# Attention and a long convolution on one core: scores in rounds of three head pairs over three double-bank buffers, and one PSUM bank for all other matrix work

## The chip, the cores and the metric

The kernel runs on one NeuronCore of a Trainium2 chip. The metric is the device time of one execution in microseconds. The kernel before took 1288.97 us (median of three runs, 1287.18 to 1289.61).

## The reference, cut to what matters

Two independent results are put side by side. The first is a state-space convolution: for each of 576 channels a kernel `K` of 2048 taps is generated from complex parameters, and the input `u` is convolved with it by a Fourier transform of double length. The second is attention with 32 query heads of width 18 over one shared key and value head.

```python
# first half (u: 2048 x 576)
P = exp(logdA[:, :, None] * l)               # logdA = dt * A, complex, 576 x 128
K = einsum("dn,dnl,dn->dl", Cc, P, dB).real  # 576 x 2048
y = irfft(rfft(u, 4096) * rfft(K, 4096))[:2048] + u * Dskip
# second half (x: 2048 x 576)
q = (x @ wq) as 32 heads of 18;  k = x @ wk;  v = x @ wv      # k, v: 2048 x 18
p = softmax(q k^T * 18 ** -0.5);  o = (p v) @ wo
return concatenate([y, o], -1)
```

## The kernel before, in words

**Attention.** The queries are split into 4 chunks of 512 (`c`), the 32 heads into 16 pairs of heads (`pr`), the keys into 16 blocks of 128 (`kb`). For one chunk, one pair and one key block, `scores` (L350) issues two matrix products, one per head, on the upper and the lower half of the TensorE rows: 55 rows of the augmented keys `kaug` against 55 rows of the augmented queries `aug`, 512 columns each, in fp32r. They write a double-bank PSUM tile `s` (128 x 1024). ScalarE turns it into `P` with one exponential (L362). Four products with `v`, fp32, each in its own 32 columns of TensorE, then add both heads of two such pairs into the accumulator `ops` (L628); each is two passes, so that a step has 8 matrix instructions on `ops`.

A **step** is two pairs of one key block: two `scores`, two exponentials, one product. There are 4 x 8 x 16 = 512 steps, and the product of a step is issued one step later, behind the scores of the next one. The pool `ps_s` holds two `s` tiles: the first pair of a step always uses one, the second the other, so that the scores of a step wait for the exponentials of the step before.

**Other TensorE work ("fills").** Query projections (`qproj`, tile `q`, ten pieces into one bank, then three VectorE instructions that read the bank), a small product for the bound on the scores (`up`), the output projection (`outproj`, `outproj_part`, tile `op`, pieces of 288 columns) use two banks of the pool `ps_q`. The convolution uses one bank of `ps_m`: `kg` (generation of the taps), `hu`, `lu`, `hk`, `lk` (forward transforms of `u` and of the taps) and `iy` (inverse transform); each tile is read by VectorE as soon as it is filled. With two double-bank `s` tiles (4 banks), one bank for `ops` (`ps_o`), two of `ps_q` and one of `ps_m`, all eight banks are in use. The convolution goes over 12 blocks of 48 channels; `front` of block k+1 (tables and taps) runs beside `back` of block k (transforms, pointwise products). Most VectorE work is the convolution's.

**Order.** The program order of TensorE, ScalarE and VectorE is fixed when the kernel is built. `Clock` holds modelled times of the three engines (`t`, `v`, `a`), the times at which the two `s` tiles are free (`s`) and the VectorE work done. Each piece of work beside the steps is a generator (`Stream`) that tells what it wants next: `"p"` a matrix product, `"v"` VectorE work, `"w"` nothing, `"b"` a moment at which ScalarE can be taken away for sines. In `main` (L578 ff.) each step issues its scores and exponentials, then lets the streams `prep`, `side` (projections) and `conv` advance as far as a `credit` in microseconds of TensorE time or the modelled idle time allows, and then issues the product of the step before. `Conv.go` holds the convolution back at `RATE` = 1.75 us of VectorE work per step.

Of the kernel before, what the change touches and what calls it, by code (L numbers as in the profile page):

```python
# [9 lines left out]
F32 = mybir.dt.float32  # L10
# [7 lines left out]
P = 128  # L18
# [13 lines left out]


RATE = 1.75
AHEAD = 0.8
# [17 lines left out]
class Clock:  # L53
# [6 lines left out]
    def __init__(self):  # L60
        self.t = self.v = self.a = 0.0
        self.work = 0.0
        self.s = [0.0, 0.0]
# [4 lines left out]
    def act(self, cost, after=0.0):  # L68
        self.a = max(self.a, after) + cost
        return self.a  # L70

# [36 lines left out]
class Stream:  # L108
# [18 lines left out]
    def go(self, step, credit):  # L127
# [22 lines left out]
class Attention:  # L150
# [7 lines left out]
    def __init__(self, tc, ctx, aps, clock):  # L158
# [22 lines left out]
    def setup(self, tp, conv):  # L181
# [8 lines left out]
        self.sel = cp.tile([P, 138], F32, name="sel_sb")  # L190
# [27 lines left out]
        nc.scalar.dma_start(self.sel, a["sel"])  # L218
# [6 lines left out]
        self.outs, self.step, self.due, self.q_free, self.scaled = [], 0, 1 << 30, [0.0, 0.0], {}  # L225
# [3 lines left out]
        kps = self.ps_q.tile([P, CT], F32, tag="q", name="kps")  # L229
        self.qps = self.ps_q.tile([P, CT], F32, tag="q", name="q0_0")  # L230
        pv = self.ps_m.tile([P, CT], F32, tag="m", name="vps")
        for k in range(5):
            for ps, j in ((kps, 0), (None, 0), (pv, 32)):
                if ps is None:
                    matmul4(nc, self.qps, self.wq[0][:, k, :], x0[:, k, :], start=(k == 0), stop=(k == 4))
                    continue
                for c in range(NCH):
                    nc.tensor.matmul(ps[32 * c:32 * c + 32, :], wkv[:, k, j:j + 32], xr[:, k, c - 1, :] if c else x0[:, k, :],
                                     start=(k == 0), stop=(k == 4), tile_position=(0, 32 * c))
        nc.scalar.activation(kh, kps, AF.Copy)  # L240
        V.tensor_reduce(km[:, 4:5], kps, axis=AX.X, op=ALU.max, apply_absolute_value=True)
        V.tensor_scalar(km[:, 0:4], self.sel[:, 134:138], km[:, 4:5], None, op0=ALU.mult)
# [12 lines left out]
        pk = self.ps_q.tile([P, 4], F32, tag="q", name="kmx")  # L255
        nc.tensor.matmul(pk[:126, :], self.sel[:, 8:134], km[:, 0:4], start=True, stop=True)
# [4 lines left out]
        vp = self.ps_m.tile([P, 4, P], F32, tag="m", name="vp")  # L261
# [9 lines left out]
    def qproj(self, c, m, xt):  # L271
# [4 lines left out]
        yield "p", max(self.q_free[0], K.t), False  # L276
        ps = self.ps_q.tile([P, CT], F32, tag="q", name=f"q{c}_{m}")
# [8 lines left out]
        yield from self.queries(c, m, ps)  # L286

    def queries(self, c, m, ps):
# [3 lines left out]
        K.v = max(K.v, K.t)  # L292
        qh = self.p2.tile([P, CT], F32R, tag="qh", name=f"qh{c}_{m}", bufs=1)
        ql = self.p2.tile([P, CT], F32R, tag="ql", name=f"ql{c}_{m}", bufs=1)
        ab = self.p2.tile([P, 1], F32, tag="ab", name=f"ab{c}_{m}")
        if (c, m) == (0, 0):
            nc.scalar.activation(qh[:mn, :], ps[:mn, :], AF.Copy)
        else:
            V.tensor_copy(qh[:mn, :], ps[:mn, :])
            V.tensor_tensor(ql[:mn, :], ps[:mn, :], qh[:mn, :].bitcast(F32), op=ALU.subtract)  # L300
        V.tensor_reduce(ab[:mn, :], ps[:mn, :], axis=AX.X, op=ALU.max, apply_absolute_value=True)
        if (c, m) == (0, 0):
            V.tensor_tensor(ql[:mn, :], ps[:mn, :], qh[:mn, :].bitcast(F32), op=ALU.subtract)
# [22 lines left out]
        yield "p", max(K.v + 0.4, self.q_free[0]), False  # L326

        up = self.ps_q.tile([P, 8], F32, tag="q", name=f"up{c}_{m}")
# [5 lines left out]
        self.q_free = self.q_free[1:] + [K.v + 0.3]  # L334
# [15 lines left out]
    def scores(self, c, pr, kb):  # L350

        nc = self.nc
# [5 lines left out]
        K = self.k  # L358
        K.pe(0.335, K.s[pr % 2])
        K.s[pr % 2] = K.act(0.925, K.t + 0.27) + 0.1  # L360
# [4 lines left out]
    def gather(self, c, g, o_ps):  # L365
        nc = self.nc
        o_sb = self.p2.tile([P, CT], F32, tag="o", name=f"o{c}_{g}")
        self.k.v = max(self.k.v, self.k.t)
        self.V.tensor_copy(o_sb, o_ps)
        nc.sync.dma_start(self.od[c][g * P:(g + 1) * P, :], o_sb)  # L370
# [37 lines left out]
    def outproj(self, c):  # L408
# [3 lines left out]
        yield "p", max(self.scaled[4], self.q_free[0]), False  # L412
        for t in range(4):
            ob = self.p1.tile([P, D], F32, tag="ob", name=f"ob{c}_{t}", bufs=2)
            for nh in range(2):
                ps = self.ps_q.tile([P, 288], F32, tag="q", name=f"op{c}_{t}_{nh}")
                for m, (m0, mn) in enumerate(MT):
                    matmul4(nc, ps, o[:mn, m, t * P:(t + 1) * P], self.wo[:mn, m, nh * 288:(nh + 1) * 288], start=(m == 0), stop=(m == 4))
# [5 lines left out]
                V.tensor_copy(ob[:, nh * 288:(nh + 1) * 288], ps)  # L424
                self.q_free = self.q_free[1:] + [K.v + 0.3]
                if nh == 0:
                    yield "p", self.q_free[0], False
            nc.sync.dma_start(self.a["outb"][c * CT + t * P:c * CT + (t + 1) * P, :], ob)
            if t < 3:
                yield "p", self.q_free[0], False  # L430

    def outproj_part(self, c, ms, part):
# [4 lines left out]
        for t in range(4):  # L437
            for nh in range(2):
                yield "p", max(self.scaled[ms[-1]], self.q_free[0]), False
                ps = self.ps_q.tile([P, 288], F32, tag="q", name=f"op{c}_{t}_{nh}_{ms[0]}")  # L440
                cs = slice(nh * 288, (nh + 1) * 288)
# [11 lines left out]
                self.q_free = self.q_free[1:] + [K.v + 0.3]  # L453

    def finish(self, c, part, o_ps, w4, b4):
# [3 lines left out]
        o_sb = self.p2.tile([P, CT], F32, tag="o", name="o_last")  # L459
        rc = self.p2.tile([P, CT], F32, tag="o", name="rc_last")  # L460
        half = [slice(f * 256, f * 256 + 256) for f in range(2)]
        cols = [slice(nh * 288, nh * 288 + 288) for nh in range(2)]
        bc = self.ps_m.tile([P, CT], F32, tag="m", name="bc")
# [14 lines left out]
        def invert(f):  # L478
            V.reciprocal(rc[:, half[f]], rc[:, half[f]])
            nc.tensor.matmul(bc[:, half[f]], b4, rc[:, half[f]], start=True, stop=True)  # L480

        def scale(f):
            V.tensor_tensor(o_sb[:, half[f]], o_sb[:, half[f]], bc[:, half[f]], op=ALU.mult)
        for nh in range(2):
            begin(0, nh, self.ps_q.tile([P, CT], F32, tag="q", name=f"fin0_{nh}"))
        for t in (1, 2):
# [18 lines left out]
        begin(3, 1, self.ps_q.tile([P, CT], F32, tag="q", name="fin3_1"))  # L505
# [6 lines left out]
    def side(self):  # L512
# [3 lines left out]
        yield from self.queries(0, 0, self.qps)  # L516
# [23 lines left out]
    def prepare(self):  # L540

        nc = self.nc
        while True:
# [11 lines left out]
            if ms[0] == 3:  # L555
                self.w4 = self.p1.tile([P, D], F32, tag="ob", name="w4", bufs=2)
# [21 lines left out]
    def main(self, conv, flag):  # L578
# [4 lines left out]
        K.t = K.v = K.a = conv.free = 0.0  # L583
        side.ready, self.q_free = 0.0, [0.0, 0.0]
        for st in conv.streams:
            st.ready = 0.0
        steps = [(c, g, kb) for c in range(NCH) for g in range(8) for kb in range(16)]
        prev, o_ps, credit, filled = None, None, 0.0, 0.0

        prep = Stream(self.prepare(), K, 99.0)  # L590

        def drain():
            while self.todo or self.busy or self.outs:
                if self.todo or self.busy:
                    prep.advance()
                if self.outs:
                    side.advance()
        for i, at in enumerate(steps + [None]):
            cur = None
            if at is not None:  # L600
                self.step = i
                c, g, kb = at
                if (g, kb) == (0, 0):
                    self.od[c] = self.dr.tile([8 * P, CT], F32, tag="od", name=f"od{c}")
                cur = [self.scores(c, 2 * g, kb), self.scores(c, 2 * g + 1, kb)]
                ready = K.act(0.0)
                credit = min(credit + min(max((TOTAL - filled) / max(LAST - i, 20), 0.45), 0.58 if i < 384 else 0.68), 0.75)
                nxt = (c, 2 * g + 3) if g < 7 else (c + 1, 1)
                more = True
                while more:  # L610
                    more, t = False, K.t

                    idle = max(K.s[0] - K.t - 0.96, K.s[1] - K.t - 1.3) - 0.15
                    order = (prep, side, conv) if self.due < i + 8 else (prep, conv, side)
                    for st in order:
                        if st.go(i, max(credit - 0.3, idle)):
                            more = True
                            break
                    filled += K.t - t
                    credit = max(credit - (K.t - t), -0.4)  # L620
# [561 lines left out]
```

## Time and profile before

| | |
|---|---|
| Runs | 1288.97, 1289.61, 1287.18 us |
| Profiled execution | 1288.89 us, span 1287.0 us |
| TensorE (PE) busy | 1223.3 us (95%) |
| ScalarE (ACT) busy | 1064.3 us (83%) |
| VectorE (DVE) busy | 991.5 us (77%) |
| Granted TensorE clock | 0.989 |

The profile gives busy times per engine, groups of instructions, waits and a timeline. In a row of the timeline the first number is the start in microseconds, the second the busy time of the instructions that are merged in the row (`x4` is four of them); a row's busy time includes the end of the pipeline, so the next row can begin before it is over. `PEld` is the loading of the stationary operand, which overlaps `PE`. In brackets stands the idle time of the engine before the row, and what ended it.

### The profile page before, as it was taken

How to read it: one execution, taken by the hardware profiler on the slowest of the kernel's cores; microseconds unless marked ns; L12 is line 12 of the kernel's file. 1: busy time of each engine (PE TensorE's matmuls, PEld its weight loads, DVE VectorE, ACT ScalarE, POOL GpSimd, SP SyncE). 2: the span in 40 equal slices, each digit the busy share in tenths (PEclk: the TensorE clock that was granted, in tenths of full speed). 3: DMA queues.
4: the chain of work that ended last, by engine and by line, in shares of the span. 5: the costliest groups of instructions: out<-in, count | busy, mean ns of one | idle time of the engine just before them, and what ended most of it. 6: DMA issues, size and time to landing. Idle time of an engine off the chain costs nothing.

```text
span 1287.0 us, 32922 instructions
## 1 busy us (share of the span) xinstructions
PE 1223.3 (95%) x13762; PEld 472.4 (37%) x13762; DVE 991.5 (77%) x1612; ACT 1064.3 (83%) x1101; POOL 227.8 (18%) x450
## 2 busy tenths in 40 slices
PE   5999999899999999999999999999899999899997
PEld 1333343243334344343334334334233334334332
DVE  4778878878878968978977976976977987786842
ACT  2689989888988888888888888888988888788884
POOL 3342102203110110231312110221302120110000
PEclk9899999899999999999999999999999999899999
DMA  7621022121120112021122011312103112021011
GB/s 224 174 70 35 17 67 65 30 75 47 53 75 23 42 58 76 25 82 51 36 75 71 29 51 42 99 33 76 31 27 107 29 40 66 13 59 64 26 39 39
DMA packets 56779, 75.35 MB, mean 59 GB/s; under 512 B 19393, under 2 KB 30017, under 8 KB 56113
## 3 DMA queue, kind: packets, MB, share of 16 engines
q1 hardware_dynamic: 35784, 58.22, 13.8%
q0 software_dynamic: 20288, 14.39, 5.1%
q8 instruction: 110, 1.80, 0.6%
q10 hardware_dynamic: 552, 0.58, 0.1%
q14 instruction: 45, 0.36, 0.1%
HBM read 35.28 MB, written 22.54 MB: 45 GB/s over the span
## 4 chain that ended last, share of the span: by engine, by line
PE 67%; issue 12%; DVE 12%; ACT 6%; POOL 1%; DMA 1%; SPq 0%; DVEq 0%; ACTq 0%; POOLq 0%
PE ops L628 24%; PE s L357 21%; ACT P L362 6%; PE op L147 5%; PE q L147 4%; PE kg L898 3%; PE iy L147 2%; DVE ks L86 2%; DVE acc L86 2%; PE lu L147 1%; PE hu L147 1%; PE hk L147 1%; PE lk L147 1%; POOL aug L321 1%; DVE f L86 1%
## 5 line engine op out<-in xcount | busy, mean ns | idle before, releaser
L362 ACT ACTIVATE P<-s 128x1024 f32<-128x1024 f32 x1024 | 985.7, 1023 | 188.7 <-PE s L357 179.3
L628 PE MATMUL ops<-P,v_sb 128*32 128x512 f32 x4096 | 548.8, 601 | 4.9 <-DVE o L90 4.6
L357 PE MATMUL s<-aug,kaug 55*128 55x512 f32 x2048 | 432.5, 475 | 38.2 <-ACT P L362 35.1
L357 PEld LDWEIGHTS s<-aug,kaug 55*128 55x128 f32 x2048 | 186.2, 185 | 543.0 <-ACT P L362 523.8
L321 POOL DMA_DIRECT2D aug<-qh x252 | 127.0, 520 | 769.0 <-DVE qh L90 394.3
L628 PEld LDWEIGHTS ops<-P,v_sb 128*32 128x32 f32 x4096 | 116.9, 110 | 90.8 <-issue 35.1
L147 PE MATMUL q<-x,wq_sb 128*32 128x256 f32 (+2 forms) x1480 | 105.9, 396 | 0.0
L147 PE MATMUL op<-wo_sb,oT 126*32 126x288 f32 (+1 forms) x1152 | 94.8, 414 | 0.0
L90 DVE COPY ksb<-kg 128x192 f32<-128x192 f32 x48 | 17.6, 366 | 83.3 <-PE kg L898 83.3
L321 POOL DMA_DIRECT2D aug<-ql x128 | 65.0, 523 | 8.4 <-issue 5.4
L86 DVE TENSOR_TENSOR tab<-tab,tt 128x576 f32<-128x576 f32 (+1 forms) x72 | 59.2, 822 | 1.8
L147 PEld LDWEIGHTS q<-x,wq_sb 128*32 128x32 f32 (+1 forms) x1480 | 42.5, 109 | 47.6 <-issue 26.3
L86 DVE TENSOR_TENSOR tab<-tab 128x576 f32<-128x576 f32 (+1 forms) x72 | 59.0, 819 | 1.0
L347 POOL DMA_DIRECT2D aug<-sh x61 | 35.2, 586 | 134.0 <-DVE sh L94 133.7
L86 DVE TENSOR_TENSOR tab<-sum,r 128x576 f32<-128x576 f32 (+1 forms) x72 | 58.9, 818 | 0.0
L86 DVE TENSOR_TENSOR tt<-f,sum 128x576 f32<-128x576 f32 (+1 forms) x72 | 58.8, 817 | 0.0
L86 DVE TENSOR_TENSOR tab<-r,dif 128x576 f32<-128x576 f32 (+1 forms) x72 | 58.8, 817 | 0.0
L86 DVE TENSOR_TENSOR sck<-lk,sck 128x384 f32<-128x384 f32 x48 | 24.5, 553 | 31.7 <-PE lk L147 31.7
L86 DVE TENSOR_TENSOR acc<-acc,pt 128x1728 f32<-128x1728 f32 (+2 forms) x36 | 48.7, 1353 | 0.2
L86 DVE TENSOR_TENSOR pt<-us,ks 128x1728 f32<-128x1728 f32 (+2 forms) x36 | 48.7, 1352 | 0.1
L86 DVE TENSOR_TENSOR u<-u,iy 128x384 f32<-128x384 f32 x24 | 13.3, 554 | 38.3 <-PE iy L147 38.3
L898 PE MATMUL kg<-tab 128*32 128x64 f32 x2304 | 42.1, 221 | 0.4 <-DVE tab L86 0.4
(118 smaller groups left out, 1003.7 us busy)
## 6 DMA issues: line engine op xcount, KB each, us to landing
aug<-qh POOLq DMA_DIRECT2D x252, 36.0 KB, 1.9
od<-o SPq DMA_DIRECT2D x31, 256.0 KB
aug<-ql POOLq DMA_DIRECT2D x128, 36.0 KB, 2.0
u<-u SPq DMA_DIRECT2D x12, 384.0 KB
kd<-ksb SPq DMA_DIRECT2D x12, 384.0 KB
kt<-kd SPq DMA_DIRECT2D x48, 96.0 KB
outa<-u SPq DMA_DIRECT2D x12, 384.0 KB
oT<-od SPq DMA_DIRECT2D x16, 252.0 KB
```

Source lines behind the costliest of these rows:

```text
L86: return self.v.tensor_tensor(out, *a, **k)
L90: return self.v.tensor_copy(out, *a, **k)
L147: nc.tensor.matmul(ps[j:e], w[:, j:e], x, start=start, stop=stop, tile_position=(0, j))
L321: q.dma_start(t[b:b + 18, :], src[r:r + 18, :])
L347: nc.gpsimd.dma_start(self.aug[(c, h // 2)][54:119:64, :], sh)
L357: nc.tensor.matmul(ps[:, j, :], self.kaug[r, kb * P:(kb + 1) * P], t[r, :], start=True, stop=True)
L362: nc.scalar.activation(pt, ps, AF.Exp, scale=SCALE)
L628: nc.tensor.matmul(o_ps[32 * j:32 * j + 32, :], self.v[:, pk, :], pts[j // 2][:, j % 2, :], start=(pk == 0), stop=(pk == 15), tile_positio ...
L898: nc.tensor.matmul(ps[32 * g:32 * g + 32, d, :], t[:, :32], t[:, 32:], start=(j == 0), stop=(j == 1), tile_position=(0, 32 * g))
```

## The change

`ps_s` gets three double-bank buffers (six banks). `ops` keeps its bank. The last bank, `ps_f`, takes every other matrix product: projections, bounds, output projection and the convolution's tiles, through the new function `bank`. `Clock.fill` is the one modelled time at which that bank is free again; it replaces `q_free` and `conv.free`. A `"p"` piece of one stream is not issued while another stream holds a half-filled bank (`holder`, `lock`).

The loop goes over 1024 pairs in rounds of three: three `scores` back to back, then the three exponentials, then the products that are due (one and two in turn: a product still takes two pairs) with fills ahead of each, then fills until the modelled time at which the next three buffers are free. Six `P` buffers take the place of four. When the convolution's VectorE work is under `PACE` = 1.68 us per step, `lags` holds back new tiles of the projections. The staging tiles `ob` (output projection) and `o` (accumulator) have one buffer where they had two. In the setup, the three projections of keys, first queries and values use the three `s` buffers, and the last two of the five parts of the values' projection come later.

```diff
+NS = 3
+NP = 6
+PACE = 1.68
...
+    def filled(self):
+        self.fill = self.v + 0.25
...
-        if not self.live or self.kind == "b" or self.kind == "p" and (credit <= 0 or k.t < self.ready):
+        if not self.live or self.kind == "b" or self.kind == "p" and (credit <= 0 or k.t < self.ready or lock not in (None, self)):
...
-        self.pp = pool("a_p", 4)
-        self.ps_s = pool("ps_s", 2, space=PSUM)
+        self.ps_s = pool("ps_s", NS, space=PSUM)
         self.ps_o = pool("ps_o", 1, space=PSUM)
-        self.ps_q = pool("ps_q", 2, space=PSUM)
-        self.ps_m = pool("ps_m", 1, space=PSUM)
+        self.ps_f = pool("ps_f", 1, space=PSUM)
+    def open(self, ctx):
+        self.pp = ctx.enter_context(self.tc.tile_pool(name="a_p", bufs=NP))
+    def bank(self, n, name):
+        return self.ps_f.tile([P, CT], F32, tag="f", name=name)[:, :n]
...
-        yield "p", max(self.q_free[0], K.t), False
-        ps = self.ps_q.tile([P, CT], F32, tag="q", name=f"q{c}_{m}")
+        yield "p", K.fill, False
+        ps = self.bank(CT, f"q{c}_{m}")
...
-        K.pe(0.335, K.s[pr % 2])
-        K.s[pr % 2] = K.act(0.925, K.t + 0.27) + 0.1
+        K.pe(cost, K.s[i % NS])
+        return ps, K.t + 0.27
+    def exponentials(self, i, c, pr, kb, ps, ready):
+        nc, K = self.nc, self.k
+        K.s[i % NS] = K.act(0.925, ready) + 0.1
...
-            ob = self.p1.tile([P, D], F32, tag="ob", name=f"ob{c}_{t}", bufs=2)
+            ob = self.p1.tile([P, D], F32, tag="ob", name=f"ob{c}_{t}")
...
+        def fill(then):
+            t = K.t
+            more = True
+            while more:
+                more = False
+                credit = state["credit"] - (K.t - t)
+                urgent = self.due < self.step + 8
+                for st in (prep, side, conv) if urgent else (prep, conv, side):
+                    if st is side and side.kind == "p" and not (urgent or side.holds) and conv.lags(self.step):
+                        continue
+                    if st.go(self.step, max(credit - 0.3, then - K.t - 0.15, 0.3 * (st is side and side.holds and conv.lags(self.step) and credit > -1.0)), holder()):
+                        more = True
+                        break
+            state["filled"] += K.t - t
+            state["credit"] = max(state["credit"] - (K.t - t), -0.4)
...
+        for r in range(0, len(pairs), NS):
+            new = range(r, min(r + NS, len(pairs)))
+            self.step = new[-1] // 2
+            ss = {}
+            for i in new:
...
+                ss[i] = self.scores(i, c, 2 * g + j, kb, 0.335 if i == r else 0.215)
+            K.t += 0.11
+            for i in new:
+                while (i - NP) // 2 >= behind:
+                    product(behind)
+                    behind += 1
+                c, g, kb, j = pairs[i]
+                pts[i] = self.exponentials(i, c, 2 * g + j, kb, *ss[i])
+                done[i] = K.a
...
+            def free():
+                return max(K.s[(r + NS + j) % NS] - 0.22 * j for j in range(NS))
+            while behind < r // 2:
+                fill(free() - 0.96 * (r // 2 - behind))
+                product(behind)
+                behind += 1
+            fill(free())
...
-            yield "p", max(tab, self.free), False
-            ps = self.ps_m.tile([P, TB // 2, 64], F32, tag="m", name=f"kg{k}_{s}_{q}")
+            yield "p", max(tab, K.fill), False
+            ps = self.bank(TB // 2 * 64, f"kg{k}_{s}_{q}").rearrange("p (d c) -> p d c", c=64)
...
+    def lags(self, step):
+        return self.work < step * PACE and any(st.live and st.kind == "p" for st in self.streams)
```

More of the change, by code (lines that the diff above doesn't have):

```diff
@@ L254, in setup @@
             self.load_wq(m)
-        pk = self.ps_q.tile([P, 4], F32, tag="q", name="kmx")
-        nc.tensor.matmul(pk[:126, :], self.sel[:, 8:134], km[:, 0:4], start=True, stop=True)
+        pk = self.bank(4, "kmx")
+        nc.tensor.matmul(pk[:126, :], spread[:, 0:126], km[:, 0:4], start=True, stop=True)
+        for k in range(3, 5):
+            project(pv, 32, k)
         V.tensor_reduce(self.kmax[:126, :], pk[:126, :], axis=AX.X, op=ALU.max)
@@ L325, in queries @@
         V.tensor_scalar(aw[:mn, :], ab[:mn, 0:1].broadcast_to([mn, P]), self.kmax[:mn, 0:1], None, op0=ALU.mult)
-        yield "p", max(K.v + 0.4, self.q_free[0]), False
-        up = self.ps_q.tile([P, 8], F32, tag="q", name=f"up{c}_{m}")
+        yield "p", max(K.v + 0.4, K.fill), False
+        up = self.bank(8, f"up{c}_{m}")
         matmul4(nc, up, aw[:mn, :], self.sel[:mn, 0:8])
@@ L437, in outproj_part @@
         for t in range(4):
[L438 to L441, printed above, removed]
+            for n in range(2):
+                yield "p", max(self.scaled[ms[-1]], K.fill), False
+                cs = slice(n * 288, (n + 1) * 288)
+                ps = self.bank(288, f"op{c}_{t}_{n}_{ms[0]}")
                 for m in ms:
@@ L479, in invert @@
             V.reciprocal(rc[:, half[f]], rc[:, half[f]])
-            nc.tensor.matmul(bc[:, half[f]], b4, rc[:, half[f]], start=True, stop=True)
+            nc.tensor.matmul(bc[f], b4, rc[:, half[f]], start=True, stop=True)
         def scale(f):
[L483 to L486, printed above, removed]
+            V.tensor_tensor(o_sb[:, half[f]], o_sb[:, half[f]], bc[f], op=ALU.mult)
+        for t in range(3):
             tile = self.ps_s.tile([P, 2, CT], F32, tag="s", name=f"fin{t}")
@@ L582, in main @@
         self.load_wo()
-        K.t = K.v = K.a = conv.free = 0.0
-        side.ready, self.q_free = 0.0, [0.0, 0.0]
+        K.t = K.v = K.a = self.o_free = 0.0
+        K.fill = 0.0
+        side.ready = 0.0
         for st in conv.streams:
             st.ready = 0.0
-        steps = [(c, g, kb) for c in range(NCH) for g in range(8) for kb in range(16)]
-        prev, o_ps, credit, filled = None, None, 0.0, 0.0
         prep = Stream(self.prepare(), K, 99.0)
[L592 to L603, printed above, removed]
-                    self.od[c] = self.dr.tile([8 * P, CT], F32, tag="od", name=f"od{c}")
[L605 to L620, printed above, removed]
-                while kb >= 12 and nxt not in self.ready and nxt[0] < NCH:
-                    side.advance()
-            if prev is not None:
-                (pc, pg, pk), pts, done = prev
-                if pk == 0:
-                    o_ps = self.ps_o.tile([P, CT], F32, tag="o", name=f"ops{pc}_{pg}")
-                for j in range(4):
-                    nc.tensor.matmul(o_ps[32 * j:32 * j + 32, :], self.v[:, pk, :], pts[j // 2][:, j % 2, :],
-                                     start=(pk == 0), stop=(pk == 15), tile_position=(0, 32 * j))
-                K.pe(0.96, done + 0.1)
-                if pk == 15 and (pc, pg) != (NCH - 1, 7):
-                    self.gather(pc, pg, o_ps)
-                    if pg == 7:
-                        self.todo.append((pc, range(5)))
-                    if pc == NCH - 1 and pg in LATE:
-                        self.todo.append((pc, LATE[pg]))
-            prev = (at, cur, ready)
@@ L638, in main, with holder, force @@
-        drain()
+        pairs = [(c, g, kb, j) for c in range(NCH) for g in range(8) for kb in range(16) for j in range(2)]
+        state = dict(credit=0.0, filled=0.0)
+        def holder():
+            return next((st for st in [side] + conv.streams if st.holds), None)
+        def force(done):
+            while not done():
+                st = holder()
+                (side if st is None else st).advance()
+        def fill(then):
[13 more added lines that the diff above has]
+            state["credit"] = max(state["credit"] - (K.t - t), -0.4)
@@ new lines, in product @@
+        def product(n):
+            nonlocal o_ps
+            c, g, kb, _ = pairs[2 * n]
+            if kb == 0:
+                fill(self.o_free)
+                o_ps = self.ps_o.tile([P, CT], F32, tag="o", name=f"ops{c}_{g}")
+            for j in range(4):
+                nc.tensor.matmul(o_ps[32 * j:32 * j + 32, :], self.v[:, kb, :], pts[2 * n + j // 2][:, j % 2, :],
+                                 start=(kb == 0), stop=(kb == 15), tile_position=(0, 32 * j))
+            K.pe(0.96, done[2 * n + 1] + 0.1, self.o_free if kb == 0 else 0.0)
+            if kb == 15 and (c, g) != (NCH - 1, 7):
+                self.gather(c, g, o_ps)
+                if g == 7:
+                    self.todo.append((c, range(5)))
+                if c == NCH - 1 and g in LATE:
+                    self.todo.append((c, LATE[g]))
@@ L639, in main @@
+        while behind < len(pairs) // 2:
+            product(behind)
+            behind += 1
+        while self.todo or self.busy or self.outs or holder():
+            if self.todo or self.busy:
+                prep.advance()
+            st = holder()
+            if st or self.outs:
+                (st or side).advance()
         conv.drain()
@@ L936, in transform @@
             for half in (1, 0):
-                yield "p", max(ready, self.free), False
-                ps = self.ps_m.tile([P, 2, NE], F32, tag="m", name=f"{'lh'[half]}{nm}{j}")
+                yield "p", max(ready, K.fill), False
+                ps = self.bank(2 * NE, f"{'lh'[half]}{nm}{j}").rearrange("p (r n) -> p r n", r=2)
                 for r in (2 * half, 2 * half + 1):
@@ L1019, in back @@
         for hf in range(2):
-            yield "p", max(ready, self.free), False
-            ps = self.ps_m.tile([P, 2, NE], F32, tag="m", name=f"iy{k}{hf}")
+            yield "p", max(ready, K.fill), False
+            ps = self.bank(2 * NE, f"iy{k}{hf}").rearrange("p (r n) -> p r n", r=2)
             sl = slice(hf * 2, hf * 2 + 2)
@@ L1066, in go @@
             return False
-        hold = any(st.holds for st in self.streams)
         for st in self.streams:
@@ L1075, in go @@
         for st in sorted(self.streams, key=lambda st: (not st.holds, st.work)):
-            if hold and st.kind == "p" and not st.holds:
-                continue
             w0 = self.k.work
-            if st.go(step, credit):
+            if st.go(step, credit, lock):
                 self.work += self.k.work - w0
@@ L1105, in build @@
             cv.open(ctx)
+            at.open(ctx)
             cv.start()
```

134 lines of the change are left out of this document (76 added, 58 removed).

## The prediction, made before the changed kernel was run

> **What bounds the kernel now.** I read the page first (busy shares, costliest groups), then the waits, then the timeline of TensorE and ScalarE in three stretches.
>
> ```profile
> PE 1223.3 (95%) x13762; PEld 472.4 (37%) x13762; DVE 991.5 (77%) x1612; ACT 1064.3 (83%) x1101; POOL 227.8 (18%) x450
> L362 ACT ACTIVATE P<-s 128x1024 f32<-128x1024 f32 x1024 | 985.7, 1023 | 188.7 <-PE s L357 179.3
> L628 PE MATMUL ops<-P,v_sb 128*32 128x512 f32 x4096 | 548.8, 601 | 4.9 <-DVE o L90 4.6
> L357 PE MATMUL s<-aug,kaug 55*128 55x512 f32 x2048 | 432.5, 475 | 38.2 <-ACT P L362 35.1
> ...
> PEld s L357 <- ACT P L362: 523.8, 717, 5.0
> ```
>
> TensorE is busy 95% of the span and ScalarE waits 179.3 us for scores: TensorE leads. But the other direction is there too: the weight load of the scores stood 523.8 us, in 717 waits, behind exponentials. Most of that passes while the product before it still streams, so it must be read step by step. Here is a step with all waits hidden, late in the loop:
>
> ```profile
> 1233.40 1.04 PE L628 MATMUL ops<-P,v_sb 128*32 128x512 f32 x8
> 1234.37 0.73 PE L357 MATMUL s<-aug,kaug 55*128 55x512 f32 x4
> 1235.04 0.86 PE L147 MATMUL iy<-w,dft_sb 128*32 128x192 f32 x16
> 1235.71 1.04 PE L628 MATMUL ops<-P,v_sb 128*32 128x512 f32 x8
> ```
>
> From start to start: product 0.97, two score pairs 0.67, fill 0.67 us. A step without stall thus costs 1.64 us and its fill. Steps without any fill take longer than that:
>
> ```profile
> 240.51 1.05 PE L357 MATMUL s<-aug,kaug 55*128 55x512 f32 x4
> 241.49 1.07 PE L628 MATMUL ops<-P,v_sb 128*32 128x512 f32 x8
> ...
> 252.57 0.51 PE L357 MATMUL s<-aug,kaug 55*128 55x512 f32 x2
> ...
> 606.01 3.77 ACT L362 ACTIVATE P<-s 128x1024 f32<-128x1024 f32 x4
> 714.07 1.94 ACT L362 ACTIVATE P<-s 128x1024 f32<-128x1024 f32 x2 [0.23 <-PE s L357]
> ```
>
> Six steps in 12.06 us are 2.01 us each. ScalarE alone would need 1.83: four exponentials last 3.77 and two 1.94, so one more costs 0.915. Neither engine is at its limit; what closes the ring is the second score buffer. The scores of the second pair wait for an exponential that itself waited for the first pair, which stood behind the product. Nothing can be computed ahead with two buffers.
>
> Over the whole loop:
>
> ```profile
> 33.01 0.76 PE L357 MATMUL s<-aug,kaug 55*128 55x512 f32 x1 [1.98 <-DMA aug<-qh]
> 1266.93 0.91 PE L357 MATMUL s<-aug,kaug 55*128 55x512 f32 x4
> ...
> 600.93 3.64 PE L147 MATMUL q<-x,wq_sb 128*32 128x256 f32 x64
> 604.39 1.04 PE L628 MATMUL ops<-P,v_sb 128*32 128x512 f32 x8
> 704.49 6.01 PE L147 MATMUL op<-wo_sb,oT 126*32 126x288 f32 x96
> 710.32 1.04 PE L628 MATMUL ops<-P,v_sb 128*32 128x512 f32 x8
> 58.33 0.88 PE L898 MATMUL kg<-tab 128*32 128x64 f32 x48 [0.37 <-DVE tab L86]
> 59.02 1.04 PE L628 MATMUL ops<-P,v_sb 128*32 128x512 f32 x8
> ...
> L147 PE MATMUL q<-x,wq_sb 128*32 128x256 f32 x1060 | 99.4, 388 | 0.0
> L147 PE MATMUL q<-x,wq_sb 128*30 128x256 f32 x300 | 78.3, 388 | 0.0
> L147 PE MATMUL q<-x,wq_sb 128*8 128x256 f32 x80 | 19.9, 385 | 0.0
> L147 PE MATMUL op<-wo_sb,oT 126*32 126x288 f32 (+1 forms) x1152 | 94.8, 414 | 0.0
> L898 PE MATMUL kg<-tab 128*32 128x64 f32 x2304 | 42.1, 221 | 0.4 <-DVE tab L86 0.4
> L147 PE MATMUL iy<-w,dft_sb 128*32 128x192 f32 x768 | 40.9, 332 | 0.0
> L147 PE MATMUL hk<-kt,dft_sb 128*32 128x192 f32 x384 | 20.8, 332 | 0.0
> L147 PE MATMUL hu<-u,dft_sb 128*32 128x192 f32 x384 | 20.6, 332 | 0.0
> ```
>
> The 511 steps between the first and the last scores take 1233.9 us. 511 x 1.64 is 838. The fills, start to start: 1440 instructions of `q` at 3.46/64 us make 77.9; 1152 of `op` at 5.83/96 make 70.0; 2304 of `kg` at 0.69/48 make 33.1; 768 of `iy` and four groups of 384 (`hk` to `hu`) at 0.67/16 make 96.5: together 277.5 us. What is left, 1233.9 - 838 - 277.5 = 118 us, is stall, 0.23 us a step, and the fill-less steps above show 0.37 of it each. So the kernel is bound by TensorE work plus a ring between TensorE and ScalarE. Setup (33 us) and tail (20 us) lie outside.
>
> **The change part by part.**
>
> *Third score pair back to back.*
>
> ```profile
> 715.80 0.50 PE L357 MATMUL s<-aug,kaug 55*128 55x512 f32 x2
> 711.29 0.76 PE L357 MATMUL s<-aug,kaug 55*128 55x512 f32 x4
> 711.90 1.94 ACT L362 ACTIVATE P<-s 128x1024 f32<-128x1024 f32 x2 [0.40 <-PE s L357]
> ```
>
> One pair is busy 0.50, two 0.73 (the row at 1234.37): a pair added directly behind another costs 0.23, while the first carries the switch. No row shows three in a row; the bounds are 0.23 and 0.335 (half of 0.67), and I take 0.23, which is the cost of an added pair as such. A round is then 0.67 + 0.23 = 0.90 against 1.5 x 0.67 = 1.005 before: 0.105 less in 341 rounds, **-36 us**. The Trainium skill ("TensorE: Matmul & The Clock Gate", Part 3, The mechanism) says that a weight load overlaps running matmuls only when their row groups differ; consecutive pairs use the same two row halves, so by it the third pair would cost the full 0.335, and the sum would be 36 us higher. The 0.23 above speaks against it.
>
> *Fewer switches from product to scores.* A product ahead of scores takes 0.97. Behind itself or a fill it should take less:
>
> ```profile
> 1230.40 0.69 PE L147 MATMUL op<-wo_sb,oT 126*32 126x288 f32 x8
> 1230.91 1.04 PE L628 MATMUL ops<-P,v_sb 128*32 128x512 f32 x8
> ```
>
> A fill of 0.69 busy gives way to a product 0.51 after its start, a tail of 0.18; the same tail off the product's 1.04 leaves 0.86. Of 512 products only 341 now stand directly ahead of scores; 171 save 0.11: **-19 us** (bounds -19 and 0).
>
> *The stall.* With three buffers the scores of a round wait for exponentials of the whole round before, and the products for exponentials that are already over: two products' worth of slack lies between. Without fill ScalarE sets the round, 3 x 0.915 = 2.75 us, against TensorE's 0.90 + 1.5 x 0.86 + 0.11 = 2.30. With the mean fill of 277.5/341 = 0.81, TensorE needs 3.11 and ScalarE no longer matters. So a stall of up to 0.45 remains in rounds with little fill. If a quarter of the rounds has none (85 x 0.45 = 38), twelve sine stretches of the convolution cost 1.5 each (18), and 0.1 is lost in each of the other 256 rounds (26), the stall is 82 of today's 118: **-36 us**. The bounds are 20 us (only the sines) and 118 plus what the shared bank adds.
>
> *One bank for all fills.* Instructions and bytes are unchanged, so nothing is added but waits: the next tile may start only when VectorE has read the last one. By the loops of the code there are 168 tiles of the convolution (48 `kg`, 96 forward, 24 inverse), which share one bank today already, 19 `q`, 20 `up` and 48 `op`. VectorE takes some 0.55 per read, three reads for `q`.
>
> ```profile
> L90 DVE COPY ksb<-kg 128x192 f32<-128x192 f32 x48 | 17.6, 366 | 83.3 <-PE kg L898 83.3
> 1240.65 0.55 DVE L86 TENSOR_TENSOR u<-u,iy 128x384 f32<-128x384 f32 x1 [3.14 <-PE iy L147]
> 40.00:1240.00 1200.00, 954.75 (x1537) 0.99 0.18 54
> ```
>
> Today it is VectorE that waits for the tile (83.3 us on `kg` alone), not TensorE for the bank. In the new order a round has two or three places for a fill, so a tile can be read behind a product. The bank would be taken for 277.5 us of filling, about 160 us of reading and, with half a microsecond of queue at VectorE for each of 255 tiles, 130 us more: half of the loop. I take 0; a wait hit by TensorE would hold back scores and products queued behind it, and through them ScalarE. Bound: 255 x 0.3 = 77 us, an estimate for the case that VectorE's queue is met every time.
>
> *The rest at nothing.* The setup's products are reordered, but the first scores wait for a DMA (1.98 us in the row at 33.01), so they are covered. `ob` and `o` with one buffer wait for a store that was issued several steps before; if that cover went, VectorE would stand until the store has landed, and the reads of the bank behind it. Six `P` buffers replace four and are read a round later. The finish uses `s` tiles for `q` tiles; same instructions.
>
> Sum: 1288.9 (profiled execution; the median of the runs, 1288.97, is the same) - 36 - 19 - 36 = **1198 us**. 0.2% is 2.6 us, about what a measurement of this kernel can tell from no change.
>
> **The rivals.**
>
> *A. The convolution is late (slower).* Its VectorE work, about 955/12 = 80 us a block with what is mixed into it, is offered per step, and the step is to shrink from 2.41 to 2.24 us; its tiles now also wait while a `q` or `op` tile is half filled. The last inverse transform came in this trace at 1240, some 11 steps ahead of the end, so there is little reserve. What isn't done by the last score is drained with nothing beside it. The gain of 91 us is used up when 1.15 blocks are left; with 1.5 blocks the time is 1198 + 120 = 1318. For it: VectorE's share rises to 955/1143 = 84% in the loop, and one bank serves both. Against: the convolution gets the bank before new projection tiles when it lags. Chance 0.23.
>
> *B. TensorE waits at the bank.* The 77 us above: 1275. The Trainium skill ("TensorEngine Tiling (Array Packing)", PSUM Bottleneck) warns that copying out of PSUM can become the limit once the matrix work is quicker. For it: the reads of `q` alone are three instructions. Against: VectorE waits for tiles today. From 1245 to 1287, chance 0.12.
>
> *C. The third pair is not cheaper.* Then only the other two terms act: 1198 + 36 = 1234. Against it the 0.73 after 0.50. Chance 0.08, inside the forecast's own band.
>
> *D. The ring was worse than I think,* and the stall goes to its lower bound of 20: 1136. Chance 0.05.
>
> **How the numbers follow.** The forecast with C, 1155 to 1245, has 0.57; B 0.12; D 0.05: faster by over 0.2% 0.74. No change 0.03, where a half of A and the gain meet. Slower 0.23. The range from 1155 to 1300 leaves out D and the longer half of A.
>
> **What would show it.** Right: rows `s` x6 of about 0.95 us; TensorE stretches of scores, one or two products and fills with a period near 3.2 us; the wait of ScalarE for scores well under 179 us; the last `iy` still ahead of the last scores. Wrong: `s` rows of three pairs over 1.1 us (C); rows in which `PE` or `PEld` of a fill waits for a VectorE read, tens of microseconds in all (B); `kg`, `hk` or `iy` rows behind the last scores, with ScalarE idle (A).

## The result: 4.5% slower, and the profile after

The changed kernel took 1346.63 us (median of four runs, 1346.04 to 1348.4) beside 1289.29 us for the kernel before: a ratio of 1.045, 95% interval 1.0432 to 1.0469. The prediction was 1198 us, with a range from 1155 to 1300: a gain was forecast, and a loss came.

The page of the changed kernel, the lines that answer to those shown of before (L390 is the exponential, L653 the product, L382 the scores):

```profile
span 1346.6 us, 32948 instructions
PE 1186.4 (88%) x13762; PEld 482.6 (36%) x13762; DVE 994.8 (74%) x1612; ACT 1044.9 (78%) x1101; POOL 225.2 (17%) x450
L390 ACT ACTIVATE P<-s 128x1024 f32<-128x1024 f32 x1024 | 966.7, 1032 | 245.3 <-PE s L382 218.8
L653 PE MATMUL ops<-P,v_sb 128*32 128x512 f32 x4096 | 543.3, 609 | 8.6 <-DVE o L99 8.6
L382 PE MATMUL s<-aug,kaug 55*128 55x512 f32 x2048 | 379.6, 451 | 62.3 <-ACT P L390 58.8
```

TensorE is busy for 37 us less (the scores alone for 53 less), and yet the span grew by 60: it now idles 160 us instead of 64. Who it waits for is in the waits of TensorE (engine, tile and line, who ended the wait; us in total, times, longest):

```profile
PE s L382 <- ACT P L390: 58.8, 118, 5.9
PE op L156 <- DVE ab L107: 18.6, 8, 3.0
PE op L156 <- DVE un L107: 7.3, 6, 2.0
PE op L156 <- DVE sck L95: 5.2, 4, 1.5
PE q L156 <- DVE sck L95: 4.7, 5, 1.6
PE up L156 <- DVE scu L95: 4.3, 3, 1.7
PE kg L965 <- DVE ab L107: 4.2, 3, 2.6
```

Before, the fills of the loop waited 0.4 us for VectorE in this view. Here the six rows above make 44.3 us, and with the smaller ones (from 4.0 down to 0.5) the sum is 67 us, 9 of them behind the last scores. A stretch of the timeline shows one of them, TensorE first, then VectorE, then ScalarE:

```profile
742.41 0.64 PE L156 MATMUL q<-x,wq_sb 128*32 128x256 f32 x8
745.28 2.58 PE L156 MATMUL op<-wo_sb,oT 126*32 126x288 f32 x24 [2.23 <-DVE ab L107]
747.56 1.94 PE L653 MATMUL ops<-P,v_sb 128*32 128x512 f32 x8
...
743.12 0.69 DVE L99 CAST qh<-q 126x512 fp32r<-126x512 f32 x1 [4.84 <-PE q L156]
743.85 0.69 DVE L95 TENSOR_TENSOR ql<-q,qh 126x512 fp32r<-126x512 f32 x1
744.46 0.68 DVE L107 TENSOR_REDUCE ab<-q 126x1 f32<-126x512 f32 x1
...
751.03 1.94 ACT L390 ACTIVATE P<-s 128x1024 f32<-128x1024 f32 x2 [6.05 <-PE s L382]
```

The last piece of the `q` tile ends at 743; its three reads by VectorE take until 745.1; the order has put an output projection tile right behind, so TensorE stands for 2.23 us, and ScalarE, whose next scores are queued behind that, for 6.05. VectorE was idle for 4.84 us ahead of it: it isn't late, the tile was placed too early. And the product at 747.56 takes 1.71 until the next row at 749.27 instead of 0.86 or 0.97: the granted clock fell after the pause (0.66 as the mean of 745 to 750).

Two more pieces lie outside the loop. At the start (ScalarE, before and after):

```profile
34.15 1.94 ACT L362 ACTIVATE P<-s 128x1024 f32<-128x1024 f32 x2 [8.38 <-DMA aug<-sh]
```

```profile
44.54 5.60 ACT L390 ACTIVATE P<-s 128x1024 f32<-128x1024 f32 x6 [19.27 <-DMA kaug<-kl]
```

and at the end (TensorE, after), where the last scores are followed by projections that wait for the bank one by one, and by the last inverse transform:

```profile
1307.54 0.50 PE L382 MATMUL s<-aug,kaug 55*128 55x512 f32 x2
...
1319.17 1.09 PE L156 MATMUL op<-wo_sb,oT 126*32 126x288 f32 x8 [0.58 <-DVE part L95]
1324.24 2.79 PE L156 MATMUL iy<-w,dft_sb 128*32 128x192 f32 x32 [3.98 <-DVE w L95]
1327.69 2.40 PE L156 MATMUL iy<-w,dft_sb 128*32 128x192 f32 x32 [0.67 <-DVE u L95]
```

From the last scores to the end it is 39 us, 20 before. The loop itself, from the first scores to the last, grew from 1234 to 1274 us.

### The profile page after: what moved, and what is told of

Same layout as the page of the kernel before. It is cut to its first block, busy times and chain, and to the rows that moved or that the text cites. A ratio compares the mean times of both kernels' runs of the same rounds, so it can differ in the third digit from the quotient of the medians.

```text
span 1346.6 us, 32948 instructions
## 1 busy us (share of the span) xinstructions
PE 1186.4 (88%) x13762; PEld 482.6 (36%) x13762; DVE 994.8 (74%) x1612; ACT 1044.9 (78%) x1101; POOL 225.2 (17%) x450
## 4 chain that ended last, share of the span: by engine, by line
PE 64%; DVE 15%; ACT 13%; issue 5%; DMA 2%; SPq 1%; ACTq 0%; DVEq 0%
PE ops L653 26%; PE s L382 18%; ACT P L390 12%; PE op L156 5%; PE q L156 5%; DVE tab L95 3%; PE iy L156 2%; PE kg L965 2%; DVE acc L95 2%; DMA xr<-xT 1%; PE hk L156 1%; DVE ks L95 1%; PE hu L156 1%; DVE f L95 1%; SPq L263 1%
## 5 line engine op out<-in xcount | busy, mean ns | idle before, releaser
L390 ACT ACTIVATE P<-s 128x1024 f32<-128x1024 f32 x1024 | 966.7, 1032 | 245.3 <-PE s L382 218.8
L653 PE MATMUL ops<-P,v_sb 128*32 128x512 f32 x4096 | 543.3, 609 | 8.6 <-DVE o L99 8.6
L382 PE MATMUL s<-aug,kaug 55*128 55x512 f32 x2048 | 379.6, 451 | 62.3 <-ACT P L390 58.8
L382 PEld LDWEIGHTS s<-aug,kaug 55*128 55x128 f32 x2048 | 175.6, 187 | 382.8 <-ACT P L390 326.9
L653 PEld LDWEIGHTS ops<-P,v_sb 128*32 128x32 f32 x4096 | 110.8, 110 | 138.6 <-issue 99.2
L156 PE MATMUL op<-wo_sb,oT 126*32 126x288 f32 (+1 forms) x1152 | 90.6, 427 | 39.5 <-DVE ab L107 18.6
L156 PEld LDWEIGHTS q<-x,wq_sb 128*32 128x32 f32 (+2 forms) x1480 | 49.7, 111 | 62.7 <-issue 37.1
L156 PEld LDWEIGHTS op<-wo_sb,oT 126*32 126x32 f32 (+1 forms) x1152 | 34.7, 112 | 92.3 <-issue 59.2
L99 DVE COPY ksb<-kg 128x192 f32<-128x192 f32 x48 | 17.4, 363 | 65.7 <-PE kg L965 65.7
L99 DVE CAST qh<-q 126x512 fp32r<-126x512 f32 (+1 forms) x19 | 13.1, 687 | 50.3 <-PE q L156 45.0
L156 PE MATMUL iy<-w,dft_sb 128*32 128x192 f32 x768 | 41.0, 347 | 8.3 <-DVE w L95 4.0
```

The lines of the kernel that those rows point to most:

```text
L99: return self.v.tensor_copy(out, *a, **k)
L156: nc.tensor.matmul(ps[j:e], w[:, j:e], x, start=start, stop=stop, tile_position=(0, j))
L382: nc.tensor.matmul(ps[:, j, :], self.kaug[r, kb * P:(kb + 1) * P], t[r, :], start=True, stop=True)
L390: nc.scalar.activation(pt, ps, AF.Exp, scale=SCALE)
L653: nc.tensor.matmul(o_ps[32 * j:32 * j + 32, :], self.v[:, kb, :], pts[2 * n + j // 2][:, j % 2, :], start=(kb == 0), stop=(kb == 15), tile ...
```

## The experiments

**The single bank, priced at one order.** Two score buffers leave banks free, so the same program order runs with one bank for fills and with two (the clock counts them as one in both; TensorE, VectorE and ScalarE get the same instructions in the same order).

The main lines of the edit of `ns2_f2`; `ns2_f1` leaves `ps_f` at 1 and gives `ps_v`, which serves two tiles of setup and finish, 2:

```diff
-NS = 3
+NS = 2
...
-        self.ps_f = pool("ps_f", 1, space=PSUM)
+        self.ps_v = pool("ps_v", 1, space=PSUM)
+
+        self.ps_f = pool("ps_f", 2, space=PSUM)
```

> The changed kernel with rounds of two pairs and two score buffers, still one bank for all fills (two small tiles of setup and finish in spare banks). If the third buffer brings what the prediction counted (36 us of score time, 19 of switches, and less stall), this is slower than the changed kernel by 50-80 us: 1400-1425. If the third buffer brings nothing, 1340-1350.

> The changed kernel with rounds of two pairs, two score buffers and two banks for fills in turn; the clock still counts them as one. If the one bank is what costs, delays of fills ended by VectorE fall from 67 to under 15 us and it is 50-70 us faster than the two-buffer kernel with one bank, near before: 1285-1320. If the new order (rounds, credit, locks) is what costs, it stays at 1340 or more.

Measured: 1375.0 us with one bank (ratio to before 1.0665, 1.0618 to 1.0712), 1311.33 with two (1.0176, 1.0148 to 1.0205). The second bank is worth 64 us. The waits of TensorE, with one bank (the longest rows of fills that VectorE ends) and with two (all rows in which it waits for VectorE within the loop):

```profile
PE op L156 <- DVE ab L107: 6.7, 3, 2.2
PE kg L969 <- DVE ab L107: 5.2, 3, 2.2
PE op L156 <- DVE sck L95: 4.9, 4, 1.2
PE iy L156 <- DVE ab L107: 4.5, 2, 2.2
```

```profile
PE ops L657 <- DVE o L99: 7.0, 9, 2.2
```

With one bank all such rows of fills make 43 us, with two none. The rest of the difference lies in pauses of 8.7 us ahead of `hk` whose end the profile doesn't explain, and in the lower granted clock (0.977 against 0.988): 0.023 of 1376.5 us less 0.012 of 1309.4 us is some 16 us, an estimate. Behind the last scores both take as long, 19.5 and 19.9 us.

The one-bank kernel is also 28 us slower than the changed kernel: the third buffer brought something there, less than its expected 50 to 80.

**The remembered time of the bank.** A stream says when its next tile may start (`ready`) when it asks; by the time it goes, another stream may have filled the bank. The edit looks the time up at the moment of going (the main lines; `outproj_part` asks in the same way):

```diff
+        if self.kind == "p" and not self.holds:
+            self.k.t = max(self.k.t, self.k.fill)
...
-        if not self.live or self.kind == "b" or self.kind == "p" and (credit <= 0 or k.t < self.ready or lock not in (None, self)):
+        if not self.live or self.kind == "b" or self.kind == "p" and (credit <= 0 or k.t < self.ready or not self.holds and k.t < k.fill or lock not in (None, self)):
...
+    def vacant(self, ready):
+        K = self.k
+        yield "p", max(ready, K.fill), False
+        while K.t < K.fill:
+            yield "p", K.fill, False
...
-        yield "p", max(self.scaled[4], K.fill), False
+        yield from self.vacant(self.scaled[4])
```

> The changed kernel, but a stream that wants to start a new tile in the shared bank looks up the bank's modelled free time at the moment it would go, not at the moment it asked (outproj asks again until it is free). Program order changes, the work does not. Theory 1, TensorE stands at the shared bank because the remembered free times are out of date (67 us of delay of fills ended by VectorE, against 4 before): those delays fall under 20 us and the time to 1290-1305 us. Rival, the bank itself is too slow for the work (VectorE's reads are late whatever the order): the delays move to other places, the time stays within 15 us of 1347.

Measured 1317.74 (1.0228, 1.0198 to 1.0257): 29 us gained, less than expected. The bank's waits in the loop went (the last two rows shown lie behind the last scores, in the drain):

```profile
PE s L384 <- ACT P L392: 81.0, 121, 7.3
PE iy L158 <- DVE w L95: 9.2, 1, 9.2
PE op L158 <- DVE part L95: 8.7, 15, 0.6
```

The loop became 53 us shorter by it (1274 to 1221), but the drain behind the last scores grew from 39 to 61 us and took back 22 of them; for 31 us of it TensorE ran at a granted clock of 0.51. The wait for exponentials rose from 58.8 to 81.0, and the granted clock fell from 0.971 to 0.958. The windows around one sine stretch show what happens in the loop (per window: PE, PEld, DVE, ACT, POOL busy, then the granted clock, DMA share, GB/s), and the timeline of TensorE in it:

```profile
700.00:721.00 21.00, 21.00 (x256) 9.12 (x252) 15.18 (x23) 18.06 (x20) 2.46 (x5) 1.00 0.23 57
721.00:728.00 7.00, 3.01 (x26) 1.31 (x22) 2.48 (x4) 6.97 (x7) 4.95 (x11) 0.90 0.29 65
728.00:733.00 5.00, 5.00 (x34) 1.38 (x32) 1.56 (x2) 2.24 (x3) 0.00 (x0) 0.50 0.00 0
```

```profile
721.16 0.86 PE L158 MATMUL lk<-kt,dft_sb 128*32 128x192 f32 x16
725.60 0.56 PE L384 MATMUL s<-aug,kaug 55*128 55x512 f32 x2 [3.59 <-ACT P L392]
...
728.16 1.94 PE L661 MATMUL ops<-P,v_sb 128*32 128x512 f32 x8
729.87 1.51 PE L158 MATMUL hk<-kt,dft_sb 128*32 128x192 f32 x16
```

While ScalarE computes sines, the bank is being read when `fill` looks, so `fill` gives up, and the next instruction in the order is a score that must wait 3.59 us. From 728 to 733 the clock is 0.50, and a product takes 1.71 (728.16 to 729.87). The Trainium skill ("TensorE: Matmul & The Clock Gate", HAM oscillation — how this bites in real kernels) gives idle gaps above some 3.4 us as the point at which the clock halves; 3.59 us agrees. Shorter pauses differ: in the changed kernel the clock fell after the 2.23 us ahead of 745.28, and it stayed at 1.00 after an equal pause ahead of 432.63. The measurement decides, so 3.4 us is no safe limit in this kernel.

**Waiting for the bank in place of giving up; priority.**

```diff
+                if not more:
+                    at = [max(st.ready, K.fill) for st in [side] + conv.streams if st.live and st.kind == "p" and not st.holds]
+                    if at and holder() is None and K.t < min(at) < then - 0.6:
+                        rest[0] += min(at) - K.t
+                        K.t = min(at)
+                        more = True
...
-PACE = 1.68
+PACE = 1.75
```

The first part stands in `fill` (time spent waiting is not taken off the credit); `fwait` has it, `pace` has both.

> The kernel with the fresh look-up of the bank, and one thing more: when nothing can go, the scores are not free yet and a tile only waits for the bank, fill moves the modelled time on to the bank's release instead of giving up. Theory, in the fresh kernel TensorE idles through the sines with fills at hand, and its granted clock then halves (113 us of the span at half clock, 31 in the kernel before): the half-clock time falls under 60 us, the scores' waits for exponentials from 120 to under 95, the time from 1318 to 1285-1300. Rival, the sines' idle time is ScalarE's and fills are lacking anyway: within 8 us of 1318.

> The fwait kernel with PACE 1.75 instead of 1.68: the projections give way earlier when the convolution lags. Theory, the tail is the late convolution: its last inverse transform comes before the last scores, the end follows the last scores by 20-25 us instead of 61 (fresh kernel), the time is 25-40 us under that of fwait. Rival, the delayed projections then stretch the loop by as much: same time as fwait within 8 us.

`fwait` took 1277.67 (0.9929, 0.9902 to 0.9956), 40 us under `fresh`: granted clock 0.981, the wait for exponentials 43.0. More than expected. `pace` took 1259.74 (0.978, 0.9761 to 0.98), another 18, under the expected 25: the loop ran 9 us longer and the tail shrank from 45 us to 19. It is faster than the kernel before and than the changed kernel. One of its sine stretches:

```profile
687.92 0.86 PE L158 MATMUL lk<-kt,dft_sb 128*32 128x192 f32 x16 [0.68 <-DVE sck L99]
690.02 2.63 PE L158 MATMUL op<-wo_sb,oT 126*32 126x288 f32 x40 [1.24 <-DVE sck L95]
692.44 1.07 PE L669 MATMUL ops<-P,v_sb 128*32 128x512 f32 x8
```

TensorE still waits at the bank, for 0.68 and 1.24, but inside a stretch in which the scores could not go anyway, and the clock stays at 1.00 from 684 to 696. Two pauses of 3.60 us are left in its loop, both ahead of the bounds' product `up`, each with the clock falling behind it (0.66 as the mean of 884 to 894, and of 1082 to 1092); the first of them:

```profile
886.54 0.30 PE L158 MATMUL up<-sel_sb,aw 126*32 126x8 f32 x8 [3.60 <-DVE aw L103]
```

**Priority alone.** The changed kernel with `PACE` 1.75 and nothing else.

> The changed kernel with PACE 1.75 and nothing else. If the late convolution is a matter of its priority alone, the last inverse transform comes ahead of the last scores and the time is 1322-1332. If it is late because the one bank is held or promised wrongly, priority doesn't help: 1340-1352.

1352.91 (1.0484, 1.0454 to 1.0513): priority gains nothing while the bank's time is wrong.

**The start.** Two ways of keeping the first `P` buffer off the tiles that the setup's DMAs still read:

```diff
# early: kh, kl, vt, ident, km allocated ahead of wkv and xr in the setup's pool
# keep:
-        kh = tp.tile([P, CT], F32R, name="kh")
+        kh = self.ring[7]
-        kl = tp.tile([P, CT], F32R, name="kl")
+        kl = self.ring[8]
```

> The changed kernel, but the setup's tiles kh, kl, vt are allocated ahead of xr, so that the first P buffers, which now lie over the setup's memory, fall on other tiles. Theory, the first exponential waits for the DMAs that still read kl, since P lies on it: the first exponential starts near 35 us instead of 44.5, the time is 1336-1340. Rival, it waits for the keys' rows that these DMAs bring: first exponential stays at 44.5, time 1347.

> The changed kernel, but kh and kl of the setup lie in two tiles of the aug ring that are not used yet, outside the setup's own memory. Theory, the first exponential waits because its P buffer lies on memory that the kaug<-kl DMAs still read: it starts near 35 us instead of 44.5, time 1336-1340 us. Rival, it waits for the keys' rows or for the whole setup pool in another way: it stays at 44.5 and the time at 1347.

> The pace kernel with kh and kl in the ring as well. If the terms add up (start -10, bank -29, sines -20, tail -35 against 1347): 1245-1265 us, faster than the kernel before. If they are the same time counted twice: 1275-1290, no better than before.

`early` changed nothing (1348.05; first exponential at 44.49, still ended by `kaug<-kl`). `keep` brought the first exponential back:

```profile
35.36 2.86 ACT L390 ACTIVATE P<-s 128x1024 f32<-128x1024 f32 x3 [10.06 <-PE s L382]
```

So the wait was for the memory, not for the keys: the scores that need the keys had run at 33.3 in the changed kernel, and only the writer of `P` stood. That reordering inside the pool didn't help says that the wait is for the setup's pool as a whole or that `P` still lay on those tiles; which, is open. The 9 us did not stay: `keep` took 1342.81, 4 us less than the changed kernel, and `best1`, with the other repairs, 1260.32, no less than `pace`. In `best1` the first scores of round two are 5.7 us ahead of `pace` (40.2 against 45.9) and the last ones 0.5 (1237.6 against 1238.1).

**What the third buffer is worth with a right clock.**

> Two score buffers and one bank for fills, with the repaired clock (fresh look-up, waiting for the bank, PACE 1.75). Theory, the third buffer's gain is the product switches and score starts of the prediction (55 us) and the ring: 1310-1330, 50-70 us slower than the three-buffer kernel with the same repairs (1260). Rival, with a right clock the third buffer is worth little and the repairs did it all: 1260-1280.

> The same with two banks for fills in turn, still counted as one. Theory, once the clock is right the second bank is worth little: within 15 us of the two-buffer kernel with one bank, against 64 us between the two before the repairs. Rival, the second bank keeps its worth: 40 us faster or more, 1260-1285.

Two buffers with all repairs took 1317.43 (1.0211, 1.0191 to 1.023) with one bank and 1314.62 (1.0194, 1.0173 to 1.0215) with two. The third buffer is worth 1317.4 - 1259.7 = 58 us, and the second bank 3 us where it had been worth 64 before the three repairs.

## Why the prediction was wrong, point by point

*The steps that held.* Three score pairs in a row are busy 0.96 us (0.95 forecast), and two products in a row go from 716.87 to 718.61 in `fresh`, 0.87 each (0.86 forecast):

```profile
716.87 1.92 PE L661 MATMUL ops<-P,v_sb 128*32 128x512 f32 x16
718.61 0.51 PE L158 MATMUL hk<-kt,dft_sb 128*32 128x192 f32 x8
719.05 0.97 PE L384 MATMUL s<-aug,kaug 55*128 55x512 f32 x6
```

Rival C is out: it would have made that row over 1.1 us. The rule of the Trainium skill that spoke for it ("TensorE: Matmul & The Clock Gate", Part 3, The mechanism) does not hold for these pairs. The two terms of 55 us fit what TensorE did in `pace`, whose busy time is 1158.8 against 1223.3 before, at a granted clock of 0.985 against 0.989. That difference does not price them alone: the rows of before count short stalls as busy (its fill-less steps of 2.01 us show no idle time).

*The step that failed: "one bank for all fills, I take 0".* It cost 64 us (same order, one bank against two, with two score buffers), near the bound of 77 that the text itself named; with three buffers the look-up alone took 53 us off the loop. The argument for 0 was that VectorE waits for tiles and that the bank is taken half the time. VectorE still waited in the changed kernel (65.7 us for `kg`), and the bank was taken for 757 of the loop's 1274 us, 0.59, counted from the first product of a tile to the end of its last read. Neither protects: TensorE, which runs in order, waits whenever one tile is placed ahead of the bank's release, whatever the mean occupancy. What placed it there was not the bank's capacity. In `pace`, which has the repaired clock, the bank was taken for even 0.68 of the loop; in the two-buffer kernel with the same repairs a second bank is worth 3 us. The diff showed it: one free time now serves streams that ask at different moments, and a stream keeps the answer it got. I read `K.fill` as if it were looked up when used. Rival B had the place and nearly the size of this term, but not the cause, and 0.12 was too little for it; the time it gave, 1245 to 1287, was 60 us short, as other steps failed too.

*The stall, forecast at -36 us,* failed as well, and came out as a rise: 58.8 us of waits for exponentials in place of 35.1, by the rows of TensorE. It did not come true behind the repairs either. The loop of `pace` lasted 1205 us; with the work terms as they stood (838 + 277.5 - 55 = 1060.5), 144 us of stall are left, the late start included, where 118 were counted before and 82 forecast. The count of sine stretches at 1.5 us each was too low, since an empty bank was assumed there too; each one could end in 3.4 to 6.8 us of half clock (745 to 750 in the changed kernel, 721 to 736 in `fresh`). In the profiled executions the mean granted clock of 0.971 over 1346.6 us, if the rest is at 1.00, is 78 us at half speed against 28 before, a loss of up to 25 us that no term of the sum had.

*The setup "at nothing"* was wrong by 10 us at its place: I covered the reordered products and overlooked that the first `P` had to wait for the setup's memory. Removing that was worth 4 us in `keep` and nothing in `best1`.

*Rival A* (the convolution late) was half right: the tail grew by 19.5 us, of which the last transforms are one part, and projections the other, which `lags` holds back while the convolution is late. It was a consequence of the bank's clock, since priority alone did nothing and priority with the right clock removed it.

*What stays open.* Two buffers with repairs and two banks (1314.6) are 25 us slower than the kernel before, which has two buffers and three banks. The start accounts for at most 10. The rest, the other order of fills or the third bank, was not separated. If the two work terms of 55 us are taken as forecast, they are nearly all of the third buffer's 58 us, and little is left for the ring, for which 36 had been forecast; the exponentials' wait is 39.2 us in `pace`, 45.0 in the two-buffer kernel with the same repairs, and 35.1 before. No run separates the two parts.

## What to carry to other kernels

When several users share one buffer, price the share by the moment at which the order was decided, not by mean occupancy: in an order that is fixed, one tile placed too early stops everything behind it on that engine. Before believing a written-out order, look for values that are remembered across other users' turns; the same order with one more buffer is the test that prices it. A repair of one wait is only worth what the next wait leaves: 29 us came from the look-up (53 in the loop, less 22 lost at the end), 40 from not standing idle in the sines, 18 from priority, and the same priority alone gave nothing.

## What the runs showed of the hardware

Not every pause of TensorE cost the clock, and not only pauses did. In the changed kernel's loop there were eight of 2.2 us: after two of them (those that end at 561.70 and 745.28) the granted clock fell to 0.50 for 3.4 us, and after six it stayed at 1.00. After all of 2.57 us and longer it was at half. In the windows (columns as above), two equal pauses that cost nothing and one that did:

```profile
430.00:440.00 10.00, 7.19 (x92) 3.07 (x88) 7.31 (x11) 8.42 (x8) 7.43 (x15) 1.00 0.34 87
1083.00:1093.00 10.00, 7.77 (x96) 3.46 (x100) 7.74 (x12) 6.33 (x8) 7.43 (x15) 1.00 0.34 86
745.00:750.00 5.00, 4.72 (x44) 2.32 (x48) 0.14 (x1) 0.00 (x0) 5.00 (x11) 0.66 0.36 77
```

Behind the last scores of the same kernel the clock fell at 1319 although no pause of the 8 us before was over 0.58; there TensorE was busy for 4.16 us of 1311 to 1319. At half clock a product took 1.71 us instead of 0.86 to 0.97. A score pair directly behind another costs 0.23 us, although both use the same row halves (rows of 0.50, 0.73 and 0.96 us for one, two and three pairs). And in this kernel the first write of `P` came 9 us later while `kh` and `kl` lay in the setup's pool than with them outside it (44.54 against 35.36).
